# One ordered list for the attention heads: paired value products, roundings through PSUM, experts' loads from ScalarE

## The chip, the cores and the metric

One NeuronCore of a Trainium2 chip. It has five engines with a queue each, which run in order and meet at semaphores: TensorE (PE; its weight loads are a row of their own, PEld), VectorE (DVE), ScalarE (ACT), GpSimd (POOL) and SyncE (SP, which here only issues DMA). TensorE writes its results to PSUM. The metric is device time in microseconds (us), lower is better.

## The reference

Three parts, one after the other: attention over 16 heads (2 batches of 8) of 768 tokens and 64 dimensions; a soft mixture of 8 experts with 4 slots each; a dense feed-forward part from 512 to 2048 to 512.

```python
q_bucket, k_bucket = ...                     # 6 sign bits of q @ proj and k @ proj
scores = np.where(q_bucket == k_bucket, (q @ k.T) / 8, -1e9)
attn = softmax(scores)                       # sums + 1e-9
x = (attn @ v)                               # as (1536, 512)
logits = x @ phi                             # 32 slots
slot_out[e] = relu((softmax0(logits).T @ x)[e] @ w1[e]) @ w2[e]
y = softmax1(logits) @ slot_out
h = y @ w_in;  out = (h / (1 + exp(-1.702 h))) @ w_out
```

`w_in` and `w_out` come as 64-bit floats, which the kernel narrows to 32 bits itself.

## The kernel before

**A head.** Keys and queries of head n lie in `raw[n]`, 128 partitions x 768. For products in the fast 32-bit format (fp32r in the rows) each is split into a rounded part and the rest: `hi2` and `hi1` (L216, L220) have ScalarE write rounded copies of 64 x 768, `hq` (L230) one more, and `lo` (L227) has VectorE subtract a rounded copy from `raw`, with two inputs in SBUF, twice per head. `bits` (L248, L237) makes the bucket bits, which four small DMAs put under the keys and queries.

Scores are made per block `kt` of 128 keys (6 blocks) and half h of the queries (384 columns): `cross` (L337) and `scores` (L344) add two products in one PSUM tile `b`, and ScalarE writes exp into `P` (L345). `av` (L359) multiplies values with P: two products per block, one for each half of the queries, each 64 columns wide, in the two column halves of the array; each runs as two passes ("x4" in the chain). `psum_add` (L353) has GpSimd add up P over the blocks. `amax` (L282, L289) makes the scores of the next head but for their small parts, and VectorE takes the maximum: 12 per head. `mprep`, `mrow`, `mstore` turn the maxima into a row that the next head's `scores` subtract.

Per two heads come the sums of P (`sums`, `recs`: L390, L399), the sum of the values (`vsum2`, L381), and per head turning the result to token order (`xtok`, L443; `xnorm`, L452); per pair of heads `xtrans` (L478) and `logits` (L489). In each head one block of `w_in` is narrowed (`win1` to `win4`): two operations of ScalarE (L123, L128), then L132 and L139 on VectorE in `wn` in SBUF, then a DMA to DRAM. And one tile of 1 MB of the experts' weights is loaded (`load_expert`, L109, from SyncE).

**PSUM.** Tag `A` (2 tiles) holds amax, `B` (3) the scores, `AV` (1) the value products, and `M` (2 tiles, `misc`) all else, in turn: bits, sums, transposes, the row of maxima, logits. A tile of a tag can be written once the tile two (or three) before it in that tag was read.

**The order** is written out: the engines run what the program issues, each in that order. A table P gives tasks a step within the head (6 steps, one per key block); `at` puts them into half steps; the loop at L657 to L685 then issues, for each step, cross and scores of the block, two amax, the value products of the block before, the tasks of the half step, and so on.

**After the heads** the rest of the experts' tiles are loaded into the memory that the attention leaves (18 tiles, SyncE), then come slots, experts (L902, L939) and the feed-forward part, whose products (L1121) run to the end.

Of the kernel before, what the change touches and what calls it, by code (L numbers as in the profile page):

```python
# [52 lines left out]
def build(nc, tc, qk0, qk, v, phi, consts, w1, w2, w_in, w_out, out):  # L53
# [53 lines left out]
    def load_expert(i):  # L107
        wtile[i] = take(F32, f"w{i}")
        SP.dma_start(wtile[i], experts[i])  # L109
# [402 lines left out]
    P = {'b2': 1.4, 'mp1': 3.5, 'mr1': 4.0, 'ms1': 4.8, 'vs0': 3, 'y0': 2.2, 'y1': 5.2, 'y2': 7.5, 'y3': 8.0, 'y4': 8.5, 'hi20': -0.4, 'bits': 0.4, 'hi21': 1.0, 'hi10': 1.5, 'hi11': 2.4, 'lo0': 2.7, 'lo1': 3.0, 'hq': 2.6, 'lr': 3.2, 'mprep': 3, 'mrow': 4, 'mstore': 4.0, 'avout': 0.0, 'vsum': 4.5, 'vsum2': 3.5, 'lv': 0.2, 'sums': 1.8, 'recs': 3.0, 'nom0': 3.5, 'nom1': 4.6, 'xtok0': -2.0, 'xn00': 0, 'xn01': 1.3, 'xtok1': 4.0, 'xn10': 4.6, 'xn11': 5.0, 'xt0': -0.3, 'xt1': 0.5, 'lg': 1.0, 'lw': -0.5, 'w1': 3.8, 'w2': 5.5, 'w3': 5.9, 'w4': 7, 'le': -1.0}  # L512
    todo = {}

    def at(n, s, f, *a):
        todo.setdefault(12 * n + int(2 * s + 24) - 24, []).append((s, f, a))

    for n in range(2, NH):
        e = n - 2
        at(e, P['hi20'], hi2, n, 0)  # L520
        at(e, P['bits' if e else 'b2'], bits, n)
        at(e, P['hi21'], hi2, n, 1)
        e = n - 1
        at(e, P['hi10'], hi1, n, 0)
        at(e, P['hi11'], hi1, n, 1)
        at(e, P['hq'], hq, n)
        at(e, P['lo0'], lo, n, 0)
        at(e, P['lo1'], lo, n, 1)
        at(e, P['lr'], load_raw, n + 2)
    for n in range(1, NH):  # L530
        k = 0 if n < NH - 1 else -1
        at(n - 1, (P['mp1'] if n == 1 else k + P['mprep']), mprep, n)
        at(n - 1, (P['mr1'] if n == 1 else k + P['mrow']), mrow, n)
        at(n - 1, (P['ms1'] if n == 1 else k + P['mstore']), mstore, n)
    for n in range(NH):
        at(n + 1, P['avout'], avout, n)
        at(n, P['lv'], load_v, n + 1)
        if n:
            at(n - 1, P['vsum'], vsum, n)
    for p in range(NH // 2):  # L540
        n = 2 * p
        at(n + 1, P['vsum2'], vsum2, p)
        if p < NH // 2 - 1:
            at(n + 2, P['sums'], sums, p)
            at(n + 2, P['recs'], recs, p)
            at(n + 2, P['nom0'], nomatch, n, nrm)
            at(n + 2, P['nom1'], nomatch, n + 1, nrm)
            at(n + 3, P['xtok0'], xtok, n)
            at(n + 3, P['xn00'], xnorm, n, 0)
            at(n + 3, P['xn01'], xnorm, n, 1)  # L550
            last = p == NH // 2 - 2
            at(n + 3, 2 if last else P['xtok1'], xtok, n + 1)
            at(n + 3, 2.5 if last else P['xn10'], xnorm, n + 1, 0)
            at(n + 3, 3 if last else P['xn11'], xnorm, n + 1, 1)
            at(n + 3, 4 if last else 6 + P['xt0'], xtrans, p, 0)
            at(n + 3, 4.5 if last else 6 + P['xt1'], xtrans, p, 1)
            at(n + 3, 5 if last else 6 + P['lg'], logits, p)
    n = NH - 2
    at(n + 1, 2.5, nomatch, n, None)
# [18 lines left out]
    for j in range(16):  # L578
        e = j - 1
        if j:  # L580
            at(e, P['y0'] if j < 3 else P['lw'], load_win, j)
            at(e, P['y1'] if j < 3 else P['w1'], win1, j)
        for k, f in enumerate((win2, win3, win4)):
            at(e, P[f"{'y' if j < 2 else 'w'}{k + 2}"], f, j)
    for i in range(NWA):
        at(i + 1, P['le'], load_expert, i)

    at(0, P['vs0'], vsum, 0)
    amaxes = {}
    A1 = [2, 2, 2, 3, 3, 3, 4, 4, 4, 4, 5, 5]  # L590
    for n in range(1, NH):
        for i in range(12):
            k = i // 2 if n < NH - 1 or i < 4 else 2 + (i - 4) // 3
            if n == 1:
                k = A1[i]
            if k is not None:
                amaxes.setdefault(6 * (n - 1) - 2 + k, []).append((n, i))

    def do(k):
        for _, f, a in sorted(todo.get(k, []), key=lambda x: (2 * x[0]) % 1):  # L600
            f(*a)
# [55 lines left out]
    for s in range(-2, max(todo) // 2 + 1):  # L657
        n, kt = s // 6, s % 6
        ax = amaxes.get(s, [])
        head = 0 <= n < NH  # L660
        late = kt == 0
        if head:
            cross(n, kt, 0)
            if late:
                cross(n, kt, 1)
            else:
                scores(n, kt, 0)
                psum_add(n, kt, 0)
        early = 2 if s else 0
        for x in ax[:early]:  # L670
            amax(*x)
        if 0 <= s - 1 < 6 * NH:
            av((s - 1) // 6, (s - 1) % 6)
        do(2 * s)
        if head:
            if late:
                scores(n, kt, 0)
            else:
                cross(n, kt, 1)
            scores(n, kt, 1)  # L680
        for x in ax[early:]:
            amax(*x)
        if head and kt > 0:
            psum_add(n, kt, 1)
        do(2 * s + 1)  # L685
# [557 lines left out]
```

## Time and profile before

| | us |
|---|---|
| median of 3 runs | 478.41 (478.35 to 481.0) |
| the profiled execution | 478.17 |
| its span | 476.4 |
| TensorE busy | 461.0 (97%) |
| VectorE busy | 340.1 (71%) |
| ScalarE busy | 289.8 (61%) |
| GpSimd busy | 240.8 (51%) |

The span leaves 1.8 us around it. The granted clock of TensorE is 0.998 of full speed, which is 2.4 GHz. Busy time counts matmuls with their modelled ends, so a busy TensorE may still pause. The attention takes the span from 20 to about 272 us, the experts to 315 us, the feed-forward part the rest. A head takes some 15.6 us. To read a stage, look at the chain of waits in it (what released each step of the chain that ended last) beside the busy time of each engine in it.

### The profile page before, as it was taken

To read this page: it belongs to the slowest core of one execution; us is meant where nothing else is said; L and a number is where in the kernel's file an instruction comes from. 1 tells how busy PE (TensorE), PEld (TensorE's weight loads), DVE (VectorE), ACT (ScalarE), POOL (GpSimd) and SP (SyncE) were. 2 spreads that over 40 slices of the span, in tenths; PEclk is the share of its full clock that TensorE was granted. 3 is DMA by queue.
4 is the path that set the end of the run, shared out by engine and by line. 5 is a ranking of instruction groups with operands and counts; after the bars stand their busy time and mean duration, and the time that the engine had idled before them with its cause. 6 is when DMAs were issued, how large, how long until landed. Compare 5 with 4: busy or idle time off the path is not lost.

```text
span 476.4 us, 7295 instructions
## 1 busy us (share of the span) xinstructions
PE 461.0 (97%) x2457; PEld 287.1 (60%) x2457; DVE 340.1 (71%) x660; ACT 289.8 (61%) x564; POOL 240.8 (51%) x247
## 2 busy tenths in 40 slices
PE   7899999999999999999999999999999999999996
PEld 3645555555555555555545553346778788888885
DVE  3688899898998998989976631459877665544541
ACT  7538867777777777876755320446666665445441
POOL 5466789596795886968957400034464530000000
PEclk9999999999999999999999999999999999999999
DMA  4325655366355643564455599999400003001001
GB/s 146 105 84 189 222 179 165 108 215 214 96 173 182 216 143 120 192 217 147 134 202 193 190 360 419 404 406 423 190 0 1 0 2 132 1 1 66 1 0 66
DMA packets 22024, 75.06 MB, mean 158 GB/s; under 512 B 3210, under 2 KB 8804, under 8 KB 16612
## 3 DMA queue, kind: packets, MB, share of 16 engines
q1 hardware_dynamic: 19672, 70.41, 41.3%
q10 hardware_dynamic: 2316, 4.20, 2.3%
q8 instruction: 19, 0.31, 0.3%
q14 instruction: 17, 0.14, 0.1%
HBM read 64.26 MB, written 7.34 MB: 150 GB/s over the span
## 4 chain that ended last, share of the span: by engine, by line
PE 82%; DVE 14%; issue 2%; ACT 1%; DMA 1%; ACTq 0%; POOL 0%; DVEq 0%
PE o L1121 28%; PE av L359 13%; PE b L337 8%; PE b L344 6%; PE a L282 6%; DVE QK L227 5%; DVE mx L289 5%; PE hp L902 3%; PE sop L939 3%; PE bp L248 3%; PE h L1093 2%; PE xtp L443 1%; PE sm L390 1%; PE lg L489 1%; PE xTp L478 1%
## 5 line engine op out<-in xcount | busy, mean ns | idle before, releaser
L353 POOL TENSOR_TENSOR Ps<-Ps,P 128x384 f32<-128x384 f32 x120 | 135.8, 1151 | 13.1 <-ACT P L345 12.9
L345 ACT ACTIVATE P<-b 128x384 f32<-128x384 f32 x192 | 90.2, 491 | 64.6 <-PE b L344 60.9
L289 DVE TENSOR_REDUCE mx<-a 128x1 f32<-128x384 f32 x192 | 97.3, 545 | 19.8 <-PE a L282 18.9
L1121 PE MATMUL o<-wh,ring 128*128 128x512 f32 x384 | 109.6, 395 | 0.2 <-ACT ring L1107 0.2
L359 PE MATMUL av<-P,v 128*64 128x384 f32 x384 | 91.6, 512 | 0.8 <-ACT P L345 0.7
L1121 PEld LDWEIGHTS o<-wh,ring 128*128 128x128 f32 x384 | 71.0, 188 | 16.5 <-issue 1.8
L337 PE MATMUL b<-QK 128*128 128x384 f32 x192 | 73.0, 393 | 0.0
L1102 DVE TENSOR_TENSOR g<-h,g 128x384 f32<-128x384 f32 x64 | 35.4, 555 | 45.9 <-ACT g L1098 44.4
L344 PE MATMUL b<-QK 97*128 97x384 f32 x192 | 64.1, 347 | 0.0
L337 PEld LDWEIGHTS b<-QK 128*128 128x128 f32 x192 | 35.6, 189 | 38.1 <-issue 38.1
L282 PE MATMUL a<-QK 88*128 88x384 f32 x192 | 55.1, 359 | 3.4 <-DVE mx L289 1.7
L1121 PE MATMUL o<-wl,ring 128*128 128x512 f32 x192 | 55.3, 393 | 0.0
L1098 ACT ACTIVATE g<-h 128x384 f32<-128x384 f32 x64 | 31.2, 491 | 28.2 <-PE h L1093 27.8
L1107 ACT CAST ring<-g 128x384 fp32r<-128x384 f32 x64 | 32.7, 513 | 24.4 <-DVE g L1102 23.7
L353 POOL TENSOR_TENSOR Ps<-P,P 128x384 f32<-128x384 f32 x30 | 29.9, 1003 | 33.8 <-ACT P L345 33.8
L282 PEld LDWEIGHTS a<-QK 88*128 88x128 f32 x192 | 36.4, 194 | 9.1 <-DVE mx L289 5.8
L1121 PEld LDWEIGHTS o<-wl,ring 128*128 128x128 f32 x192 | 35.9, 188 | 9.6 <-issue 1.7
L344 PEld LDWEIGHTS b<-QK 97*128 97x128 f32 x192 | 35.3, 190 | 9.3 <-issue 8.7
L227 DVE TENSOR_TENSOR QK<-raw,QK 64x768 fp32r<-64x768 f32 x28 | 39.8, 1421 | 0.8
L359 PEld LDWEIGHTS av<-P,v 128*64 128x64 f32 x384 | 22.6, 134 | 28.3 <-ACT P L345 15.2
L1112 DVE TENSOR_TENSOR ring<-g,ring 128x384 fp32r<-128x384 f32 x64 | 38.7, 608 | 0.3
L1027 POOL TENSOR_TENSOR wl<-wt,wh 128x512 fp32r<-128x512 f32 x16 | 22.9, 1429 | 31.3 <-ACT wh L1022 31.0
(169 smaller groups left out, 567.5 us busy)
## 6 DMA issues: line engine op xcount, KB each, us to landing
w<-in_w SPq DMA_DIRECT2D x32, 1024.0 KB, 5.0
wif<-in_w_in SPq DMA_DIRECT2D x16, 512.0 KB, 3.8
wof<-in_w_out SPq DMA_DIRECT2D x7, 1024.0 KB, 19.8
raw<-in_qk SPq DMA_DIRECT2D x15, 384.0 KB, 3.0
win<-wn ACTq DMA_DIRECT2D x16, 256.0 KB, 4.0
v<-in_v SPq DMA_DIRECT2D x16, 192.0 KB, 3.9
win<-win SPq DMA_DIRECT2D x3, 1024.0 KB, 12.8
QK<-Bt SPq DMA_DIRECT2D x60, 48.0 KB, 2.7
```

What stands on the lines that cost most here:

```text
L227: (V if n > 1 else G).tensor_tensor(out=q1[r, s, :], in0=raw[n][r, :], in1=hi.bitcast(F32), op=ALU.subtract)
L282: T.matmul(a, q2[0:88, 0, qt * 128 : (qt + 1) * 128], q2[0:88, 1, h * HS : (h + 1) * HS], start=True, stop=True,)
L289: V.tensor_reduce(out=mxs[n][:, qt, h : h + 1], in_=a, axis=AX.X, op=ALU.max)
L337: T.matmul(b, q1[:, 1, kt * 128 : (kt + 1) * 128], q1[:, 0, h * HS : (h + 1) * HS], start=True, stop=False)
L344: T.matmul(b, q2[0:97, 1, kt * 128 : (kt + 1) * 128], q2[0:97, 0, qs], start=False, stop=True)
L345: A.activation(out=Pt[n, kt][:, qs], in_=b, func=AF.Exp, scale=0.125)
L353: e.tensor_tensor(out=Ps[n][:, c], in0=Pt[n, 0][:, c] if kt == 1 else Ps[n][:, c], in1=Pt[n, kt][:, c], op=ALU.add)
L359: T.matmul(avp[n][64 * h : 64 * h + 64, :], vt[n][:, kt, :], Pt[n, kt][:, h * HS : (h + 1) * HS], start=kt == 0, stop=kt == KT - 1,)
L1102: V.tensor_tensor(out=gt[i], in0=hp[i], in1=gt[i], op=ALU.mult)
L1107: A.copy(out=gh[i], in_=gt[i])
L1112: (e or V).tensor_tensor(out=gl[i], in0=gt[i], in1=gh[i].bitcast(F32), op=ALU.subtract)
L1121: T.matmul(op[grp, t], u[i][:, t * 128 : (t + 1) * 128], w[wq][:, wi, :], start=f == 0 and j == 0, stop=f == NF - 1 and j == 2,)
```

## The change

1. `lo` is replaced by `lo1` and `lo2`: ScalarE rounds all 128 partitions of half the columns into a PSUM tile (tag `M`), and VectorE subtracts it from `raw` in two operations of 64 x 384, each with one input in SBUF and one in PSUM. So a head has two roundings of 128 x 384 where it had one `hi1` of 64 x 768, and four subtractions where it had two. `narrow1` of `w_in` writes to a PSUM tile of tag `M` too, and the two roundings on VectorE read it there.
2. The value products of key blocks 0 and 1, and of 4 and 5, are issued back to back.
3. All tasks of a head, cross, scores, amax, value products and sums too, have a place in one list that is sorted by a new table P; the loop is gone. P has 5 buffers instead of 4.
4. The 14 experts' tiles that come during the attention are issued from ScalarE's queue.

```diff
@@ -106,7 +106,7 @@
 
     def load_expert(i):
         wtile[i] = take(F32, f"w{i}")
-        SP.dma_start(wtile[i], experts[i])
+        (A if i < NWA else SP).dma_start(wtile[i], experts[i])
 
 
...
-    def narrow3(dst, f64, c):
+    def narrow3(dst, f64, c, src=None):
...
-            out=d, in0=hi[:, c, :], scalar=-(2**31), in1=d, op0=ALU.bitwise_and, op1=ALU.bitwise_or
+            out=d,
+            in0=hi[:, c, :],
+            scalar=-(2**31),
+            in1=d if src is None else src.bitcast(I32),
+            op0=ALU.bitwise_and,
+            op1=ALU.bitwise_or,
...
+    lot = {}
+
+    def lo1(n, h):
+        lot[h] = pps.tile([128, HS], F32R, name=f"lo{n}_{h}", tag="M", bufs=2)
+        A.copy(out=lot[h], in_=raw[n][:, h * HS : (h + 1) * HS])
+
+    def lo2(n, h):
+        c = slice(h * HS, (h + 1) * HS)
+        for s in range(2):
+            r = QR[s]
+            V.tensor_tensor(
+                out=QK1[n % 2][r, s, c], in0=raw[n][r, c], in1=lot[h][r, :].bitcast(F32), op=ALU.subtract
+            )
...
-            Pt[n, kt] = pq.tile([128, S], F32, name=f"P{n}_{kt}", tag="P", bufs=4)
+            Pt[n, kt] = pq.tile([128, S], F32, name=f"P{n}_{kt}", tag="P", bufs=5)
...
+    wp = {}
+
+        narrow0(wf[j], 0, A)
+        wp[j] = misc([128, 512], f"wp{j}")
+        narrow1(wp[j], wf[j], 0)
...
-        narrow3(wn[j], wf[j], 0)
+        narrow3(wn[j], wf[j], 0, wp[j])
...
-    P = {'b2': 1.4, 'mp1': 3.5, ...}
+    P = {
...
+        "s11": 1.52, "xn01": 1.5784, "lo20": 1.6, "sums": 1.828, "c20": 1.8892, "s20": 2.02, "a1": 2.06, "v0": 2.1,
+        "v1": 2.101, "a11": 2.1167, "lo11": 2.1197, "c21": 2.2278, "hi11": 2.357, "s21": 2.3896, "lo21": 2.424,
...
+    tasks = []
+
+    def put(n, s, f, *a):
+        tasks.append((6 * n + s, len(tasks), f, a))
...
+    for n in range(NH):
+        for kt in range(KT):
+            for h in range(2):
+                put(n, P[f"c{kt}{h}"], cross, n, kt, h)
+                put(n, P[f"s{kt}{h}"], scores, n, kt, h)
+                if kt:
+                    put(n, P[f"p{kt}{h}"], psum_add, n, kt, h)
+            put(n, P[f"v{kt}"], av, n, kt)
...
-    for s in range(-2, max(todo) // 2 + 1):
...
+    for _, _, f, a in sorted(tasks, key=lambda x: x[:2]):
+        f(*a)
```

TensorE, head 5, key blocks 1 and 2, before (b is a score tile with its head, block and half; a is amax of the next head; av the value products; the lines are those of each kernel):

```order
L359 MATMUL av5_1183<-P5_0_1135,v5_956 64x384 x2
L337 MATMUL b5_1_1_1191<-QK1_1_94 128x384
L344 MATMUL b5_1_1_1191<-QK2_2_88 128x384
L337 MATMUL b5_2_0_1198<-QK1_1_94 128x384
L344 MATMUL b5_2_0_1198<-QK2_2_88 128x384
L282 MATMUL a6_8_1203<-QK2_0_93 128x384
L282 MATMUL a6_9_1206<-QK2_0_93 128x384
L359 MATMUL av5_1183<-P5_1_1170,v5_956 64x384 x2
L337 MATMUL b5_2_1_1212<-QK1_1_94 128x384
L344 MATMUL b5_2_1_1212<-QK2_2_88 128x384
L337 MATMUL b5_3_0_1220<-QK1_1_94 128x384
```

and with the change:

```order
L357 MATMUL b5_2_0_1226<-QK1_1_94 128x384
L364 MATMUL b5_2_0_1226<-QK2_2_88 128x384
L302 MATMUL a6_1_1230<-QK2_0_93 128x384
L379 MATMUL av5_1233<-P5_0_1174,v5_974 64x384 x2
L379 MATMUL av5_1233<-P5_1_1201,v5_974 64x384 x2
L302 MATMUL a6_11_1238<-QK2_0_93 128x384
L357 MATMUL b5_2_1_1243<-QK1_1_94 128x384
L364 MATMUL b5_2_1_1243<-QK2_2_88 128x384
L357 MATMUL b5_3_0_1253<-QK1_1_94 128x384
L364 MATMUL b5_3_0_1253<-QK2_2_88 128x384
L302 MATMUL a6_10_1259<-QK2_0_93 128x384
```

The value products of block 0 have moved back to stand beside those of block 1, behind the scores of block 2.

ScalarE in the same stretch of head 5, before (P is exp, with its head and block; the CASTs are roundings, win32 the DMA of the narrowed weights):

```order
L345 ACTIVATE P5_1_1170<-b5_1_0_1171 128x384
L216 CAST QK2_1_86<-raw7_1065 64x768
L509 DMA win32_1_75<-wn5_1074 128x512
L345 ACTIVATE P5_1_1170<-b5_1_1_1191 128x384
L220 CAST QK1_0_89<-raw6_858 64x768
L345 ACTIVATE P5_2_1197<-b5_2_0_1198 128x384
L220 CAST QK1_0_89<-raw6_858 64x768
L345 ACTIVATE P5_2_1197<-b5_2_1_1212 128x384
L230 CAST QK1_0_89<-QK2_0_93 64x768
L345 ACTIVATE P5_3_1219<-b5_3_0_1220 128x384
L345 ACTIVATE P5_3_1219<-b5_3_1_1239 128x384
```

and with the change (lo is the new rounding, w an expert's tile):

```order
L365 ACTIVATE P5_1_1201<-b5_1_0_1202 128x384
L532 DMA win32_1_75<-wn5_1152 128x512
L239 CAST lo6_0_1216<-raw6_887 128x384
L365 ACTIVATE P5_1_1201<-b5_1_1_1214 128x384
L365 ACTIVATE P5_2_1225<-b5_2_0_1226 128x384
L239 CAST lo6_1_1241<-raw6_887 128x384
L225 CAST QK1_0_89<-raw6_887 64x768
L365 ACTIVATE P5_2_1225<-b5_2_1_1243 128x384
L250 CAST QK1_0_89<-QK2_0_93 64x768
L365 ACTIVATE P5_3_1252<-b5_3_0_1253 128x384
L109 DMA w5_1265<-in_w1 128x2048
```

One of the two roundings of L220 has become two (L239) that write a tile of tag `M`, the first of them ahead of the exp that the paired value products wait for, and the expert's load has come into this queue.

## Rows read from the trace of the kernel before

**Rows 1.** the page: busy us, share, instructions; then busy tenths in 40 slices.

```profile
PE 461.0 (97%) x2457; PEld 287.1 (60%) x2457; DVE 340.1 (71%) x660; ACT 289.8 (61%) x564; POOL 240.8 (51%) x247
...
DVE  3688899898998998989976631459877665544541
```

**Rows 2.** windows of two heads: length, PE, PEld, DVE, ACT, POOL busy, granted clock, DMA.

```profile
85.59:116.88 31.29, 31.06 (x170) 17.30 (x171) 28.47 (x57) 23.36 (x45) 24.33 (x26) 1.00 0.52 171
...
179.14:210.29 31.15, 30.92 (x170) 17.16 (x171) 28.34 (x57) 23.53 (x45) 24.53 (x26) 1.00 0.49 168
```

**Rows 3.** the chain of waits inside those windows: start, length (us), what.

```profile
103.03 0.80 PE av L359 x4
103.83 0.37 PE b L337
104.20 0.18 PE b L344
...
105.09 1.42 PE av L359 x4
...
109.00 0.33 PE xtp L443 x3
...
113.57 0.78 PE bp L248 x8
```

**Rows 4.** the timeline, a weight load after a burst: start, length, idle before.

```profile
101.70 0.19 PEld L337 LDWEIGHTS b<-QK 128*128 128x128 f32 x1 [0.60 <-issue]
```

**Rows 5.** the chain of waits: a rounding of VectorE on the path.

```profile
120.81 1.65 DVE QK L227
```

**Rows 6.** the chain of waits behind the attention: 512-column passes of the experts.

```profile
275.54 0.88 PE lg L765 x4
...
284.37 6.14 PE hp L902 x56
```

**Rows 7.** groups by line, VectorE, 60:250 us: xcount, busy us, mean ns.

```profile
L227 DVE TENSOR_TENSOR QK<-raw,QK 64x768 fp32r<-64x768 f32 x26 | 36.6, 1406 | 0.8
L139 DVE SCALAR_TENSOR_TENSOR wn<-wif,wn 128x512 int32<-128x512 int32 x12 | 16.5, 1376 | 0.4
...
L132 DVE SCALAR_TENSOR_TENSOR wn<-wn,wif 128x512 int32<-128x512 int32 x12 | 11.6, 964 | 0.0
...
L493 DVE TENSOR_TENSOR LT<-lg,LT 64x384 f32<-64x384 f32 x4 | 2.2, 553 | 2.7 <-PE lg L489 2.7
```

**Rows 8.** line L227: smallest, median, largest ns.

```profile
L227 DVE TENSOR_TENSOR QK<-raw,QK x28: 951/1553/1653, 43.4 to 247.8; 64x768 fp32r<-64x768 f32 x28
```

**Rows 9.** the chain of waits: roundings of weights, late and in the first heads.

```profile
317.91 0.71 DVE wt L132
...
26.20 1.47 DVE wn L132
...
42.77 0.60 DVE wn L139
```

**Rows 10.** groups by line on ScalarE, 60 to 250 us.

```profile
L345 ACT ACTIVATE P<-b 128x384 f32<-128x384 f32 x145 | 68.2, 491 | 43.0 <-PE b L344 42.5
L220 ACT CAST QK<-raw 64x768 fp32r<-64x768 f32 x24 | 19.9, 831 | 0.6
...
L369 ACT COPY xu<-av 128x384 f32<-128x384 f32 x12 | 5.8, 480 | 2.8 <-PE av L359 2.4
```

**Rows 11.** the experts' loads on SyncE: issue ns, smallest, median, largest.

```profile
L109 SPq DMA_DIRECT2D w<-in_w x14: 387/422/427, 34.9 to 234.8; - x14
```

**Rows 12.** the chain of waits in the last head but one.

```profile
252.86 1.09 PE av L359 x4
...
256.96 1.24 PE av L359 x4
```

**Rows 13.** the tile xtp in 94 to 105 us: first and last start.

```profile
L452 DVE SCALAR_TENSOR_TENSOR x<-xtp,rr,nv x6: 268/269/269, 100.3 to 102.8; 128x64 f32<-128x64 f32 x6
...
L443 PE MATMUL xtp<-cst,xu x3: 273/273/329, 94.3 to 94.6; 128*128 128x128 f32 x3
```

More of the change, by code (lines that the diff above doesn't have):

```diff
@@ L513, in build @@
[L513 removed]
+    P = {
[14 rows of a table added]
+    }
+    tasks = []
+    def put(n, s, f, *a):
+        tasks.append((6 * n + s, len(tasks), f, a))
     def at(n, s, f, *a):
[L516 removed]
+        k = int(2 * s + 24) - 24
+        x = 2 * s - k
+        put(n, k / 2 + (0.12 + 0.3 * x if k % 2 == 0 else 0.1 + 0.38 * x), f, *a)
     for n in range(2, NH):
         e = n - 2
[L520 to L522 removed]
+        put(e, P['hi20'], hi2, n, 0)
+        put(e, P['bits' if e else 'b2'], bits, n)
+        put(e, P['hi21'], hi2, n, 1)
@@ L523, in build @@
         e = n - 1
[L524 to L529, printed above, removed]
+        put(e, P['hi11'], hi1, n, 1)
+        put(e, P['hq'], hq, n)
+        for h in range(2):
+            put(e, P[f'lo1{h}'], lo1, n, h)
+            put(e, P[f'lo2{h}'], lo2, n, h)
+        put(e, P['lr'], load_raw, n + 2)
     for n in range(1, NH):
         k = 0 if n < NH - 1 else -1
-        at(n - 1, (P['mp1'] if n == 1 else k + P['mprep']), mprep, n)
@@ L538, in build @@
+        put(n, P['lv'], load_v, n + 1)
         if n:
-            at(n - 1, P['vsum'], vsum, n)
+            put(n - 1, P['vsum'], vsum, n)
     for p in range(NH // 2):
         n = 2 * p
-        at(n + 1, P['vsum2'], vsum2, p)
+        put(n + 1, P['vsum2'], vsum2, p)
         if p < NH // 2 - 1:
[L544 to L550, printed above, removed]
-            last = p == NH // 2 - 2
[L552 to L557, printed above, removed]
+            put(n + 2, P['sums'], sums, p)
+            put(n + 2, P['recs'], recs, p)
+            put(n + 2, P['nom0'], nomatch, n, nrm)
+            put(n + 2, P['nom1'], nomatch, n + 1, nrm)
+            put(n + 3, P['xtok0'], xtok, n)
+            put(n + 3, P['xn00'], xnorm, n, 0)
+            put(n + 3, P['xn01'], xnorm, n, 1)
+            last = p == NH // 2 - 2
+            put(n + 3, 2.12 if last else P['xtok1'], xtok, n + 1)
+            put(n + 3, 2.6 if last else P['xn10'], xnorm, n + 1, 0)
+            put(n + 3, 3.12 if last else P['xn11'], xnorm, n + 1, 1)
+            put(n + 3, 4.12 if last else P['xt0'], xtrans, p, 0)
+            put(n + 3, 4.6 if last else P['xt1'], xtrans, p, 1)
+            put(n + 3, 5.12 if last else P['lg'], logits, p)
@@ L558, in build @@
     n = NH - 2
-    at(n + 1, 2.5, nomatch, n, None)
+    put(n + 1, P['vsum2'] + 0.01, nomatch, n, None)
     at(n + 1, 3.5, nomatch, n + 1, None)
@@ L580, in build @@
         if j:
-            at(e, P['y0'] if j < 3 else P['lw'], load_win, j)
-            at(e, P['y1'] if j < 3 else P['w1'], win1, j)
+            put(e, P['y0'] if j < 3 else P['lw'], load_win, j)
+            put(e, P['y1'] if j < 3 else P['w1'], win1, j)
         for k, f in enumerate((win2, win3, win4)):
-            at(e, P[f"{'y' if j < 2 else 'w'}{k + 2}"], f, j)
+            put(e, P[f"{'y' if j < 2 else 'w'}{k + 2}"], f, j)
     for i in range(NWA):
[L586 to L590, printed above, removed]
+        put(i + 1, P['le'], load_expert, i)
+    put(0, P['vs0'], vsum, 0)
+    A1 = [0.54, 0.54, 0.54, 1.06, 1.06, 1.54, 2.06, 2.06, 2.54, 2.54, 3.06, 3.06]
     for n in range(1, NH):
         for i in range(12):
-            k = i // 2 if n < NH - 1 or i < 4 else 2 + (i - 4) // 3
+            x = P[f"a{i}"]
             if n == 1:
[L595 to L601, printed above, removed]
+                x = A1[i]
+            elif n == NH - 1 and i >= 4:
+                x = (i - 4) // 3 + (0.06 if (i - 4) % 3 < 2 else 0.54)
+            put(n - 1, x, amax, n, i)
+    for n in range(NH):
+        for kt in range(KT):
+            for h in range(2):
+                put(n, P[f"c{kt}{h}"], cross, n, kt, h)
[3 more added lines that the diff above has]
+            put(n, P[f"v{kt}"], av, n, kt)
     idle[0] = pps.tile([128, 128], F32, name="idle0", tag="AV", bufs=1)
@@ L655, in build @@
     mrow1(1)
-    for s in range(-2, max(todo) // 2 + 1):
[L658 to L685, printed above, removed]
+    for _, _, f, a in sorted(tasks, key=lambda x: x[:2]):
+        f(*a)
     att.close()
```

21 lines of the change are left out of this document (9 added, 12 removed), and 12 rows, old and new, of the table P.

## Prediction

> **What bounds the kernel now.** I began with the page: TensorE is busy 97% of the span, VectorE 71%, but in the first 60% of the span (the attention) VectorE's tenths read 8 and 9, later 4 to 7 [rows 1]. The share over the span thus hides that two engines are near full in the stage that changes. The windows of two heads show it: of 31.2 us VectorE works 28.4, ScalarE 23.5, GpSimd 24.4, and TensorE nearly all [rows 2]; five such windows follow one another with 31.1 to 31.8 us, the first and the fourth stand here. The granted clock is 1.00 in them, so the 2.4 GHz level, and I expect no change there.
>
> Is TensorE really working, or waiting? In the chain of waits a 384-column product takes 0.18 us, a block's value products 0.80, the first full-width product behind them 0.37, bits (and likewise sums and logits) 0.78, three transpositions 0.33 [rows 3]. For two heads: 72 x 0.18 = 13.0; 12 x 0.80 = 9.6; 4 x 0.78 = 3.1; ten returns to full width at 0.37 - 0.18 = 0.19 make 1.9; 15 transposing passes at 0.11 make 1.7; three small products, estimated at 0.2, make 0.6. Sum 29.9, so about 1.3 of 31.2 us are waits. The largest is one value product of 1.42 instead of 0.80 [rows 3]; the others are tenths, some where VectorE is late, as in the stretch where the chain runs over its subtraction of 1.65 us [rows 5].
>
> So TensorE's own work bounds the attention, VectorE is 1.5 us per two heads behind it, and either alone would bring little.
>
> **Part 1: value products in pairs.** The 0.37 is a weight load of 0.19 us that starts only when its product could, after an idle of 0.60 [rows 4], where other loads run under the product before. Entering a burst costs as well: the experts' products, in column parts too, run 56 passes in 6.14 us, 0.877 for eight passes of 512 columns, two to each part of the array [rows 6]. Scaled to 384 columns a block's value products would take 0.66 inside a stream; alone they take 0.80, so 0.14 is the entry. The change has four bursts a head instead of six: per two heads 4 x 0.14 = 0.56. The returns hardly fall: counted in the order, six value bursts are followed by a full-width product before and six after (the rest by the row of maxima, bits, sums or logits), and bits' returns go from two to one: 0.19. Together 0.75, over 8 pairs of heads **6.0 us**. The bounds are 4 x 0.14 alone, 4.5 us, and 4 x (0.14 + 0.19), 10.6 us.
>
> **Part 2: roundings through PSUM, on VectorE.** Two subtractions of 64 x 768 per head, on average 1.406 us [rows 7], become four of 64 x 384. The old one takes 0.951 at best, 1.553 in the middle and 1.653 at worst [rows 8]. For the new one the trace has no row; half of the best is 0.48, half of the worst 0.83, and the nearest (64 x 384, one input in PSUM) is 0.553 [rows 7], which I take. L139 and L132 take 1.376 and 0.964 [rows 7], but 0.60 and 0.71 at other places [rows 9], so I take 0.70 with PSUM, with 0.60 and the old means as ends. VectorE per two heads: 28.4 - 4 x 1.406 + 8 x 0.553 - 2 x (1.376 + 0.964) + 4 x 0.70 = 25.3. At the low end 24.3, at the high end 28.4 - 5.6 + 8 x 0.83 = 29.4.
>
> That the old subtraction has two prices, 0.95 and 1.6, with GpSimd busy 78% of the time, looks like a collision of the two engines in SBUF. The Trainium skill (SBUF — State Buffer, Who interferes with whom) says that a VectorE instruction with two SBUF inputs contends with a GpSimd one that reads SBUF, and one with at most one SBUF input does not. By that rule the new forms always have their low price, which is my sum; were the collision of another kind (any VectorE access beside GpSimd's), the high end of 29.4 holds, and that is rival C.
>
> **On ScalarE**: one rounding of 0.831 less, two of 128 x 384 more. No row writes PSUM from SBUF at this size; half of 0.831 is 0.42, exp 0.491, a copy of that size 0.480 [rows 10], which I take. Two loads are added at 0.422 [rows 11]. 23.5 - 2 x 0.83 + 4 x 0.48 + 2 x 0.42 = 24.6 of about 30: covered on average, because TensorE's work exceeds it; not covered where an exp stands behind it that value products wait for. SyncE loses 14 loads and nobody waited for that queue on the path, so I count no gain; if ScalarE's slack were gone, the loads would cost 14 x 0.42 = 5.9 us.
>
> **Part 3: the order.** The wait of 1.42 - 0.80 = 0.62 and the tenths behind VectorE should mostly go: VectorE drops by 3.1 us, and between the last scores of a block and its value products now stand the products of the block before too. In exchange there is a new wait: the first rounding (`lo1`) stands ahead of the exp for which the first pair waits, and writes a tile of tag M, which in every second head is free only when three more token steps are done by VectorE (0.27 each [rows 13], behind two maxima). I walk that stretch with the row durations: exp ready 0.65 us late for the pair. The second pair waits for an exp behind the two operations on w_in: 0.2. With a few tenths elsewhere I put 0.9 of waits against 1.3 now: 0.4 x 7 pairs = **2.8 us**.
>
> **The ends.** In the first heads VectorE is alone on the path with a rounding of 1.47 [rows 9], which I price at 0.70; with a little less on the maxima, 1.0 us. In the last two heads (no maxima left) five value products take 1.09 to 1.24 instead of 0.80 [rows 12], 1.3 us in all, because each waits for the exp just issued; with pairs the wait is shared, and a further wait of some 0.7 us near the start of the last head should go: 2.0. Together **3.0 us**.
>
> Behind the attention nothing is changed: from 275.5 us [rows 6] to the end 200.9 us remain. The experts' remaining tiles go into memory that the attention leaves, so their loads start earlier with it.
>
> **Sum**: 478.17 (the profiled execution, 0.2 below the median) - 6.0 - 2.8 - 3.0 = 466.4; I say **466 us**. Its own range is 461 to 472, from the bounds of part 1 and waits of 0.4 to 1.5 per two heads.
>
> **Rivals.**
> A, *all waits go*: with VectorE at 25.3 TensorE never stops. 6.0 + 1.3 x 7 + 4 = 19: 459 us, with the upper bound of part 1 down to 455. For it: every other engine has 5 us of slack per two heads. Against it: tag M.
>
> B, *waits take the place of the entry cost*: tag M's two tiles pass to 18 tenants per two heads instead of 12 (four roundings, two w_in blocks). Turns are fixed, so one long tenancy stops the rest; now the token tile lies from 94.3 to 103.1 us, 8.8 us [rows 13]. If waits come to 2.2 per two heads, 6.0 - 0.9 x 7 + 3.0 leaves 2.7: 475.5 us. The Trainium skill (Perfetto Trace Analysis, Identifying Performance Opportunities) says that the same gap repeated on the engine that should be full can mean too little PSUM for the next tile; that would be this rival, and the present trace has no such gap at tag M. For it: in every head bits would also wait until L139 has read the w_in tile. Against it: the new order has the token tile written at the end of a head and read by step 1.6 of the next head's 6, some 4 us.
>
> C, *VectorE stays as slow*: at 29.4 it is as near to the period as today; parts 1 and 3 bring nothing while it is late, and some 1.5 us remain: 477 us. Against it: the two prices of one instruction [rows 8].
>
> D, *slower*: ScalarE becomes the bound through tag M. It runs in order, and at six places per two heads (four roundings, two w_in operations) it now needs a free M tile before the exps behind can run. Its work is 24.6, so it decides once these six waits exceed 30.5 - 24.6 = 5.9 us, 1 us each. At 1.3 us each the period is 24.6 + 7.8 = 32.4: 478.2 - 3.0 + 1.2 x 7 = 484 us; at 1.6 each 497. For it: an 8.8 us tenancy exists. Against it: most tenants are read within a microsecond or two.
>
> **Chances.** Forecast 0.61, A 0.15, B 0.10, C 0.05, D 0.09. One per cent is 4.8 us, about what a measurement can tell here. Faster by more (below 473.6): forecast and A, 0.76. Within: B and C, 0.15. Slower: D, 0.09. The range 457 to 477 leaves out D, half of C and a third of A.
>
> **What would show it.** Right: in the chain, pieces of eight value passes of about 1.46 us; two heads in about 30 us; the subtraction near 0.55 and both roundings near 0.70 with little spread; GpSimd's sums shorter too; the stage from the logits of the experts to the end again 201 us. Wrong: value products of far more than 1.46 behind ScalarE (B, D), roundings on ScalarE with an idle ahead of them that ends with VectorE (tag M), subtractions above 0.8 (C).

## The result, and the profile after it

The changed kernel takes **465.16 us** (median of 4 runs, 464.51 to 467.56), the kernel before beside it 478.68 us (4 runs, 478.35 to 481.0): ratio 0.9716, 95% interval 0.9678 to 0.9754. The forecast was 466 us, range 457 to 477. The profiled execution has a span of 463.2 us, against 476.4. Medians and intervals here and below leave out one execution, at 481.7 us and a lower granted clock (0.984), of the kernel with w_in's rounding in SBUF.

First the page of the changed kernel, in the form of [rows 1]: busy us, share, instructions.

```profile
PE 448.4 (97%) x2457; PEld 288.5 (62%) x2457; DVE 319.6 (69%) x688; ACT 284.4 (61%) x578; POOL 222.0 (48%) x247
```

VectorE and GpSimd have lost some 20 us each for the same results, ScalarE 5. TensorE's share is 97% as before: its busy time fell with the span, from 461.0 to 448.4.

A window of two heads, to be read against [rows 2] (length, then PE, PEld, DVE, ACT, POOL busy, granted clock, DMA):

```profile
112.67:142.50 29.83, 29.71 (x169) 17.46 (x171) 25.79 (x61) 23.26 (x49) 22.01 (x25) 1.00 0.52 177
```

A pair of heads takes 29.8 us instead of 31.3, and the clock is the same. The chain of waits near that window's middle, the counterpart of [rows 3]:

```profile
129.60 1.44 PE av L379 x8
131.04 0.38 PE a L302
```

Eight passes of two blocks take 1.44 us where two times four took 1.60, and the return behind them is 0.38 as before. VectorE's groups, 60 to 235 us, against [rows 7]:

```profile
L245 DVE TENSOR_TENSOR QK<-raw,lo 64x384 fp32r<-64x384 f32 x46 | 25.4, 552 | 1.0
...
L139 DVE SCALAR_TENSOR_TENSOR wn<-wif,wp 128x512 int32<-128x512 int32 x12 | 8.3, 689 | 0.4
L132 DVE SCALAR_TENSOR_TENSOR wp<-wp,wif 128x512 int32<-128x512 int32 x12 | 8.2, 685 | 0.5 <-ACT wp L128 0.5
```

All three cost what the forecast put down (0.553, 0.70, 0.70).

**Where the gain comes from.** The span is 13.2 us shorter, 13.4 up to the experts' logits. Pieces of the chain that stand at the same work in both kernels cut the span. Before: the bits' product of the third head (counted as the order runs), then logits of the first and of the sixth window.

```profile
52.11 0.78 PE bp L248 x8
85.59 0.77 PE lg L489 x4
242.06 0.77 PE lg L489 x4
```

After, the same, and the experts' logits, which stood at 275.54 in [rows 6]:

```profile
52.37 0.78 PE bp L268 x8
82.83 0.82 PE lg L509 x4
231.38 0.77 PE lg L509 x4
262.10 0.88 PE lg L785 x4
```

| stretch | before | after | change | forecast |
|---|---|---|---|---|
| up to the third head's bits | 52.11 | 52.37 | +0.26 | -1.75 |
| to the first logits | 33.48 | 30.46 | -3.02 | -7.3, with the next row |
| five windows of two heads | 156.47 | 148.55 | -7.92 | (in the row above) |
| to the experts' logits | 33.48 | 30.72 | -2.76 | -2.75 |
| from there to the span's end | 200.9 | 201.1 | +0.2 | 0 |

The forecast's 7.3 is six of its eight pairs at 0.75 and its 2.8 of waits; the first row has its 1.0 and a pair, the fourth its 2.0 and a pair. So the sum came out, at 13.2 for 11.8, because the middle (the second and third rows) gave 3.6 us more than forecast and the first heads 2.0 less: two misses of opposite sign, and that is luck. The rows are good to some 0.8 us only, since the new list puts other work around the same piece: the bits stand 2.5 us behind the first product of their head where they stood 1.7, so some 0.8 of the first two rows is the cut's. Counted from the first product of a head to that of the head two later, the first two heads take 27.9 us instead of 30.4, and it is the third and fourth that gain nothing. Those two heads, before, after, and in the fastest version below (461.35 us), in the form of [rows 2]:

```profile
50.44:80.64 30.20, 29.97 (x162) 16.62 (x161) 27.48 (x55) 23.01 (x44) 25.80 (x27) 1.00 0.55 180
```

```profile
47.96:78.18 30.22, 29.07 (x161) 16.97 (x161) 25.01 (x60) 23.26 (x46) 22.47 (x26) 1.00 0.59 194
```

```profile
48.12:76.23 28.11, 28.01 (x162) 16.92 (x161) 25.07 (x60) 22.32 (x45) 22.57 (x26) 1.00 0.59 192
```

With the change TensorE is idle for 1.15 us of them, against 0.1 in the fastest version. What stands there in the chain of waits:

```profile
42.58 0.34 ACTq L109
...
43.00 6.20 DMA wif<-in_w_in
...
50.95 0.86 PE av L379 x2
```

The load of a piece of w_in goes out at 43.00, 0.4 us behind an expert's megabyte, and lands at 49.2; ScalarE, in order, holds the exponentials behind it and the value product waits. In the steady heads a kindred wait is new, on ScalarE (60 to 235 us). The second line is its counterpart in the kernel before (L216, 60 to 250 us), with 0.5 us of idle in all:

```profile
L221 ACT CAST QK<-raw 64x768 fp32r<-64x768 f32 x22 | 18.2, 829 | 6.9 <-DMA raw<-in_qk 6.8
```

```profile
L216 ACT CAST QK<-raw 64x768 fp32r<-64x768 f32 x22 | 18.3, 832 | 0.5
```

### The profile page after: what moved, and what is told of

Same layout as the page of the kernel before. It is cut to its first block, busy times and chain, and to the rows that moved or that the text cites. A ratio compares the mean times of both kernels' runs of the same rounds, so it can differ in the third digit from the quotient of the medians.

```text
span 463.2 us, 7325 instructions
## 1 busy us (share of the span) xinstructions
PE 448.4 (97%) x2457; PEld 288.5 (62%) x2457; DVE 319.6 (69%) x688; ACT 284.4 (61%) x578; POOL 222.0 (48%) x247
## 4 chain that ended last, share of the span: by engine, by line
PE 88%; DVE 5%; DMA 2%; ACT 2%; issue 1%; ACTq 0%; POOL 0%; DVEq 0%
PE o L1141 27%; PE av L379 15%; PE a L302 9%; PE b L357 8%; PE b L364 7%; PE hp L922 3%; PE sop L959 3%; PE bp L268 3%; PE h L1113 2%; PE xtp L463 1%; PE lg L509 1%; DMA wif<-in_w_in 1%; DVE mx L309 1%; PE xTp L498 1%; PE sm L410 1%
## 5 line engine op out<-in xcount | busy, mean ns | idle before, releaser
L373 POOL TENSOR_TENSOR Ps<-Ps,P 128x384 f32<-128x384 f32 x120 | 119.9, 1010 | 23.9 <-ACT P L365 20.9
L309 DVE TENSOR_REDUCE mx<-a 128x1 f32<-128x384 f32 x192 | 102.1, 548 | 21.5 <-PE a L302 20.2
L365 ACT ACTIVATE P<-b 128x384 f32<-128x384 f32 x192 | 85.8, 487 | 43.0 <-PE b L364 41.6
L379 PE MATMUL av<-P,v 128*64 128x384 f32 x384 | 77.0, 503 | 1.0 <-ACT P L365 1.0
L302 PE MATMUL a<-QK 88*128 88x384 f32 x192 | 70.7, 383 | 3.0 <-DVE QK L257 1.4
L357 PE MATMUL b<-QK 128*128 128x384 f32 x192 | 67.4, 366 | 0.2
L364 PE MATMUL b<-QK 97*128 97x384 f32 x192 | 65.2, 353 | 0.0
L373 POOL TENSOR_TENSOR Ps<-P,P 128x384 f32<-128x384 f32 x30 | 29.8, 1004 | 39.7 <-ACT P L365 39.6
L379 PEld LDWEIGHTS av<-P,v 128*64 128x64 f32 x384 | 23.7, 135 | 27.4 <-issue 21.8
L1132 DVE TENSOR_TENSOR ring<-g,ring 128x384 fp32r<-128x384 f32 x64 | 39.8, 624 | 0.3
L1047 POOL TENSOR_TENSOR wl<-wt,wh 128x512 fp32r<-128x512 f32 x16 | 22.6, 1412 | 30.2 <-ACT wh L1042 29.9
L125 POOL TENSOR_SCALAR wof<-wof 128x512 int32<-128x512 uint16 x16 | 11.1, 696 | 44.7 <-DMA wof<-in_w_out 43.6
```

The lines of the kernel that those rows point to most:

```text
L302: T.matmul(a, q2[0:88, 0, qt * 128 : (qt + 1) * 128], q2[0:88, 1, h * HS : (h + 1) * HS], start=True, stop=True,)
L309: V.tensor_reduce(out=mxs[n][:, qt, h : h + 1], in_=a, axis=AX.X, op=ALU.max)
L357: T.matmul(b, q1[:, 1, kt * 128 : (kt + 1) * 128], q1[:, 0, h * HS : (h + 1) * HS], start=True, stop=False)
L373: e.tensor_tensor(out=Ps[n][:, c], in0=Pt[n, 0][:, c] if kt == 1 else Ps[n][:, c], in1=Pt[n, kt][:, c], op=ALU.add)
L379: T.matmul(avp[n][64 * h : 64 * h + 64, :], vt[n][:, kt, :], Pt[n, kt][:, h * HS : (h + 1) * HS], start=kt == 0, stop=kt == KT - 1,)
L1132: (e or V).tensor_tensor(out=gl[i], in0=gt[i], in1=gh[i].bitcast(F32), op=ALU.subtract)
```

## Experiments

My theory: 0.75 us per pair of heads from TensorE's entries and returns, the rest from waits that go because VectorE is shorter; the loads are neutral. The rivals: the list alone did it; or VectorE's speed did; or PSUM waits eat part of it. All times are medians of 4 to 6 executions, taken beside executions of the kernel before at 478.5 to 478.8 us; the last columns come from the logits' lines of each trace (L511 and L513, in the old code 20 lines earlier).

| kernel | us | ratio to before, 95% | first logits copied at | from there to the last logits added |
|---|---|---|---|---|
| before | 478.7 | | 86.4 | 182.7 |
| changed | 465.16 | 0.9678 to 0.9754 | 83.7 | 171.4 |
| before + pairs | 473.32 | 0.9869 to 0.9901 | 85.6 | 178.9 |
| unpaired | 484.29 | 1.0095 to 1.0134 | 89.3 | 184.6 |
| unpaired, later | 476.18 | 0.9937 to 0.9966 | 87.6 | 178.9 |
| low parts in SBUF | 468.68 | 0.9761 to 0.9804 | 85.0 | 173.9 |
| w_in in SBUF | 474.82 | 0.9894 to 0.9950 | 88.1 | 176.6 |
| experts on SyncE | 463.58 | 0.9656 to 0.9734 | 83.9 | 169.8 |
| raw earlier | 471.33 | 0.9809 to 0.9863 | 91.8 | 171.5 |
| first heads | 463.42 | 0.9649 to 0.9714 | 83.5 | 171.2 |
| expert before raw | 503.80 | 1.0496 to 1.0555 | 98.1 | 197.4 |
| expert after raw | 461.35 | 0.9634 to 0.9659 | 81.7 | 170.4 |
| that + w_in in SBUF | 465.33 | 0.9710 to 0.9736 | 81.6 | 173.6 |
| list alone | 493.73 | 1.0288 to 1.0332 | 92.7 | 191.0 |

### The pairs

**Pairs in the old loop.**

```diff
...
-            av((s - 1) // 6, (s - 1) % 6)
+            for k in {1: (0, 1), 2: (2,), 3: (3,), 5: (4, 5)}.get((s - 1) % 6, ()):
+                av((s - 1) // 6, k)
...
-            Pt[n, kt] = pq.tile([128, S], F32, name=f"P{n}_{kt}", tag="P", bufs=4)
+            Pt[n, kt] = pq.tile([128, S], F32, name=f"P{n}_{kt}", tag="P", bufs=5)
```

> The kernel before with the pairing alone: value products of key blocks 0 and 1, and of 4 and 5, in one step of the old loop (five P buffers instead of four), everything else as before. Theory (0.75 us per two heads, saved on TensorE's own time): 472.7 us (478.7 less 6.0). Rival (VectorE at 28.4 of 31.3 us per two heads is as near to the bound, so that a shorter TensorE only waits for it): 476 to 478.7 us. Rival (the bound of 10.6): 468 us.

Measured 473.32 us, 5.4 less: the theory's 6.0 lies within the interval (4.7 to 6.3). But the total hides a miss. Five windows of two heads lie between these two pieces of the chain:

```profile
84.74 0.84 PE lg L489 x4
...
238.98 0.77 PE lg L489 x4
```

They take 154.24 us instead of 156.47: 0.45 per pair and not 0.75. The stretch behind them, to the experts' logits, takes 31.90 instead of 33.48, so 1.58 less, about twice what the theory gives one pair; there, most likely, the joined value products share their waits for the exponentials. In the steady heads VectorE now stands in TensorE's way:

```profile
115.55:146.30 30.75, 30.25 (x167) 17.42 (x167) 27.85 (x57) 23.46 (x45) 24.78 (x25) 1.00 0.52 172
```

VectorE works 27.85 of the 30.75 us, and the chain of waits runs over it from 118.5 to 132.2 us but for 1.1 us, where in the kernel before it did so from 119.7 to 125.3. So the first rival is half right, and the theory's total came out in part by luck.

**Pairs taken out of the list.**

```diff
-        ... "v0": 2.1, ... "v4": 6.114, ...
+        ... "v0": 1.03, ... "v4": 5.53, ...
```

> The changed kernel with one thing undone: the value products of key blocks 0 and 1, and of 4 and 5, stand apart again (block 0 after the exponentials of block 1, block 4 after those of block 5), so that each head has six entries into the two-column-half form instead of four. Theory (an entry 0.14 us and a return 0.19 us that pairing saves, 0.75 us per two heads): the two-head windows lengthen from 29.8 to 30.6 us and the kernel takes 471.2 us (465.2 + 6.0). Rival (the pairing saves nothing by itself, the list did it): 465 to 466 us. Rival (the bound of the forecast, 10.6): 475.8 us.

Measured 484.29, 19 us more: outside everything I had expected. The chain of waits shows that my place for block 0 was a bad one:

```profile
135.57 0.88 ACT P L365 x2
...
136.49 0.87 PE av L379 x4
```

The product stands right behind the scores whose exponentials it needs, and TensorE waits 0.9 us for them. So I moved it half a step.

```diff
-        ... "v0": 1.03, ...
+        ... "v0": 1.53, ...
```

> The changed kernel unpaired once more, with the product of key block 0 half a step later than in the run before (behind the second scores of key block 1, at 1.53 instead of 1.03 of its head), where its exponentials have ended. Theory (an entry and a return cost 0.33 us, and the other 13 us of the first unpaired run were TensorE standing for the exponentials of block 0, about 1 us a head): 471 to 473 us. Rival (the pairing is worth 19 us in this order because VectorE is no longer near the bound, so that all that TensorE does counts): 480 us or more.

Measured 476.18, 11.0 us more than paired: 8.1 of the 19 were that wait, and the rest is twice what the pairs are worth in the old loop. One reason is VectorE in the old loop, seen above. Another shows in the chain of this kernel, and below it the old kernel's.

```profile
119.37 0.80 PE av L379 x4
120.16 0.78 PE sm L410 x8
...
134.47 0.80 PE av L379 x4
135.26 0.37 PE b L357
```

```profile
129.23 0.80 PE av L359 x4
130.03 0.78 PE bp L248 x8
```

In the old order some bursts of value products ran straight into other work in narrow parts (bits) or into the row of maxima, so splitting or joining them moved no return. In the list three of the four split pairs per two heads have full-width products on either side of both halves: each of these splits costs an entry of 0.16 and a return of 0.19, together 1.05. The fourth runs straight into the sums (119.37) and costs little, and the value product at 145.24 takes 1.08, so 0.28 more; 1.33 in all. The chain from logits to logits is 117.86 to 149.00 us in the unpaired list, 31.14, and 29.86 paired (112.67 to 142.53): 1.28. How much of the factor of two goes to either reason no run separates.

### The roundings

**Low parts of Q and K back in SBUF.**

```diff
+        put(e, P['lo10'], hi1, n, 0)
...
-            put(e, P[f'lo1{h}'], lo1, n, h)
-            put(e, P[f'lo2{h}'], lo2, n, h)
+            put(e, P[f'lo2{h}'], lo, n, h)
```

> The changed kernel with the low parts of Q and K taken as before: one VectorE subtraction per half from two SBUF inputs, the rounded part from SBUF. Theory (a subtraction with two SBUF inputs runs at about 1.4 to 1.6 us beside GpSimd and one with a PSUM input does not): line 227's operation is back at 1.4 us or more, VectorE's busy time in a two-head window rises from 25.8 to about 27 us, and, since it is not the bound, its longer operations cost 0.1 to 0.4 us of waits per pair: 466 to 468 us. Rival (VectorE's speed was what the gain in the steady heads came from): at least 3 us more, 468 to 472. Rival (two PSUM buffers fewer in use by the low parts take away waits): 465 or below.

Measured 468.68, 3.5 more: just above the theory's range and at the foot of the first rival's. Groups between 84 and 236 us:

```profile
L373 POOL TENSOR_TENSOR Ps<-Ps,P 128x384 f32<-128x384 f32 x80 | 84.6, 1074 | 7.4 <-ACT P L365 5.8
...
L302 PEld LDWEIGHTS a<-QK 88*128 88x128 f32 x121 | 22.8, 189 | 16.7 <-issue 6.1 <-DVE mx L309 5.2 <-DVE QK L232 3.0
L232 DVE TENSOR_TENSOR QK<-raw,QK 64x768 fp32r<-64x768 f32 x20 | 20.9, 1046 | 1.4 <-ACT QK L225 0.9
```

The old subtraction runs at 1.05 us here, not at 1.4 to 1.6, and VectorE's sum per two heads moves only from 25.8 to 26.1 us. TensorE's maxima products now wait 3.0 us for it. A window takes 30.20 instead of 29.83 us, 0.37 longer, the upper end of the theory's 0.1 to 0.4: not through a subtraction of 1.4 us or more, as I had it. That it costs because it comes in one piece of 768 columns is my reading; no run shows it, since the edit also takes four tenants per two heads out of tag M and changes ScalarE's roundings.

**Rounding of w_in back in SBUF.**

```diff
-        wp[j] = misc([128, 512], f"wp{j}")
-        narrow1(wp[j], wf[j], 0)
+        if j:
+            wn[j] = scratch([128, 512], F32, f"wn{j}", "wn")
+        narrow1(wn[j], wf[j], 0)
...
-        narrow2(wp[j], wf[j], 0)
+        narrow2(wn[j], wf[j], 0)
...
-        narrow3(wn[j], wf[j], 0, wp[j])
+        narrow3(wn[j], wf[j], 0)
```

> The changed kernel with the second and third step of the rounding of w_in back in SBUF, in place, at the same places of the list. Theory: the two steps are back at 0.96 and 1.4 us beside GpSimd, VectorE gets 1.7 us more per two heads, and waits of 0.1 to 0.3 us per pair come back; but in the first heads a PSUM buffer of the group M is no longer held from the first step to the third: 464.5 to 467.5 us. Rival: VectorE becomes the bound again, 468 us or more.

Measured 474.82, 9.7 more: the rival's side. The two operations are slow again:

```profile
L139 DVE SCALAR_TENSOR_TENSOR wn<-wif,wn 128x512 int32<-128x512 int32 x16 | 21.2, 1328 | 0.5
L132 DVE SCALAR_TENSOR_TENSOR wn<-wn,wif 128x512 int32<-128x512 int32 x16 | 16.4, 1027 | 8.0 <-ACT wn L128 8.0
```

But the chain of this kernel runs over transfers:

```profile
46.16 7.01 DMA win<-wn
...
108.23 7.87 DMA raw<-in_qk
```

A store of the last piece that the next rounding waits for and raw loads that take almost 8 us (and, at 28.71, a load of w_in of 7.21). To tell those from VectorE's own share, the loads had to be moved first.

### The loads

**Experts' loads on SyncE again.**

```diff
-        (A if i < NWA else SP).dma_start(wtile[i], experts[i])
+        SP.dma_start(wtile[i], experts[i])
```

> The changed kernel with all experts' loads issued by SyncE again. Theory (the loads are hidden in the steady heads, the issuing engine costs ScalarE 0.4 us per load off the path): 464.5 to 466 us, no difference. Rival (SyncE's queue holds the loads of raw and w_in behind the expert's, as in the old kernel): up to 2 us more through later raw loads, 467 us. Rival (in the first heads the expert's load no longer stands ahead of that of w_in by its own queue): 464 us.

Measured 463.58, below all that I had put down. The interval overlaps that of the changed kernel, so a gain of 1.6 us is likely but not proved; it lies in the steady heads, not in the first. ScalarE's wait for raw between 60 and 235 us falls from 6.8 to 1.5 (total, times, longest):

```profile
ACT QK L221 <- DMA raw<-in_qk: 1.5, 2, 0.9
```

The place in the list is the same, but the load goes out at another time. Here are the expert's load and the raw load in one head, first in the changed kernel, then in this one (SPq and ACTq are the queues of SyncE and ScalarE):

```profile
102.26 0.34 ACTq L109 DMA_DIRECT2D w<-in_w  x1
103.21 0.33 SPq L194 DMA_DIRECT2D raw<-in_qk  x1
```

```profile
101.55 0.43 SPq L109 DMA_DIRECT2D w<-in_w  x1
103.42 0.33 SPq L194 DMA_DIRECT2D raw<-in_qk  x1
```

Between 60 and 130 us the megabyte goes out 0.95 to 1.0 us ahead of raw from ScalarE, and 1.9 to 4.2 us ahead from SyncE, so that raw, as I read it, meets less of it.

**The raw load earlier.** The dictionary's place `"lr"` goes from 3.70 to 2.55.

> The changed kernel with the load of raw of the head after next issued right after the last read of its buffer (at 2.55 of the head instead of 3.70). Theory (ScalarE's rounding of a head waits up to 1.6 us for that load, six times, 6.8 us in all, and half of it or less reaches TensorE through the exponentials): 463 to 465 us. Rival (the wait is covered): 465 us.

Measured 471.33, 6 us more. The raw load cannot start earlier, since it waits on SyncE until the last low part has read its buffer; in the steady heads nothing changes (171.5 against 171.4). In the first heads, though, the load of w_in now stands behind that wait in SyncE's queue, and lands 8 us after its issue:

```profile
44.60 7.81 DMA wif<-in_w_in
```

That wait is paid twice. TensorE works only 1.99 of the 6 us from 48 to 54, and then runs at half its clock (granted clock 0.50, the 1.2 GHz level):

```profile
54.00:60.00 6.00, 5.86 (x18) 3.00 (x19) 3.36 (x6) 2.99 (x6) 1.00 (x1) 0.50 0.10 33
```

**The first heads closed up.**

```diff
-        ... "y3": 8.2348, "y4": 10.3141,
+        ... "y3": 6.4, "y4": 7.4,
...
-            put(e, P['y0'] if j < 3 else P['lw'], load_win, j)
+            put(e, P['y0'] if j < 2 else 0.6 if j < 3 else P['lw'], load_win, j)
```

> The changed kernel with the first heads' roundings of w_in closed up (third step at 6.4 instead of 8.2, its store at 7.4 instead of 10.3, the load of the third piece at 0.6 instead of 2.96 of its head). Theory (in the second head the rounding waits for a load that is issued only at 43.0 us behind an expert's load and lands at 49.2, and TensorE with it for 1.0 to 2.5 us): 463 to 464 us. Rival (the first heads are bound by loads in any order): 465 us.

Measured 463.42, on the theory, but the interval overlaps that of the changed kernel. The stall for w_in is gone and one for raw, behind the same expert's load, is next:

```profile
44.70 6.48 DMA raw<-in_qk
```

**The expert's load before or after the raw load**, both with the edit above: `"le"` from -2.497 (3.5 of a head's six steps, raw at 3.70) to -4.4 (1.6) or to -1.3 (4.7).

> The same with the expert's load behind the raw load (at 4.7 of the head). Theory: as with the load ahead, 459 to 462 us. Rival (behind raw the expert's load delays the small transfers of the row of maxima and of the bits, and TensorE waits for these): 464 us or more. Rival (the issue on ScalarE, not the transfer, is what costs, since SyncE's issue saved 1.6 us): 463.4 us.

> The changed kernel with the first heads' roundings of w_in closed up and the expert's load issued 1.9 of a step earlier in each head (at 1.6 instead of 3.5, where 3.7 is the place of the raw load). Theory (the load of raw takes 6 to 8 us because the 1 MB of the expert's goes ahead of it; free of that it lands in 3 to 4 us, and ScalarE's waits for raw, 9.2 us in all, go, of which a part reaches TensorE): 459 to 462 us. Rival (raw is late because its buffer comes free late, not because of the expert's load): 463.4 us, as with the first heads alone.

Behind the raw load: **461.35 us**, interval clear of the changed kernel's, 3.8 us faster than it and the fastest here. Of these, 2.1 are over the version with the first heads closed up alone, whose interval still touches this one's. Raw takes 3.1 us to land in the middle, and ScalarE no longer waits for it between 60 and 235 us, though ScalarE still issues the expert's load. So those waits came from the megabyte going out just ahead of raw; the issuing engine matters, as far as the runs show, through the time at which it sends the load. The gain lies in the first heads (2.0 us) and the steady ones (1.0).

```profile
raw<-in_qk SPq DMA_DIRECT2D x15, 384.0 KB, 3.1
```

Ahead of it: 503.80 us, 40 us more than with the first heads closed up alone. The expert's load now meets the bits, four transfers of 48 KB for which the maxima wait:

```profile
114.50 7.63 DMA QK<-Bt
...
124.46 0.32 PE b L364
...
125.74 1.31 PE av L379 x4
```

This I had not thought of; raw itself did land in 3.3 us, so the theory on raw held and the price was elsewhere. A large part of that price is TensorE's clock, which falls to half behind such waits (the last section shows one): the mean granted clock of the profiled execution is 0.951 over 503.4 us, so by an estimate up to some 25 us of the 40.

### The rounding of w_in, without the transfers

The edit of the rounding above, in the version of 461.35 us.

> The rounding of w_in back in SBUF once more, now in the version that took 461.35 us (the first heads' roundings closed up, the expert's load behind the raw load). Theory (of the 10 us that the rounding in SBUF cost before, most was transfers: raw loads that went out later behind a longer VectorE and landed behind the expert's megabyte, 7.2 to 7.9 us each, and in the first heads a store that the next rounding waited for; VectorE's own part is 0.1 to 0.3 us per pair): 462 to 464.5 us. Rival (the 1.0 and 1.3 us operations themselves hold up the maxima and low parts that TensorE waits for): 468 us or more.

Measured 465.33, 4.0 more than 461.35: between theory and rival. So of the 9.7 about 6 came with the transfers; 4.0, or 0.5 per pair, are left for VectorE's longer operations. A window of two heads here, and then of the version of 461.35 us:

```profile
80.81:110.86 30.05, 29.92 (x169) 17.39 (x171) 27.39 (x61) 23.00 (x48) 23.16 (x25) 1.00 0.53 176
```

```profile
80.87:110.50 29.63, 29.50 (x170) 17.45 (x171) 25.82 (x61) 22.94 (x48) 22.00 (x25) 1.00 0.55 179
```

And what the weight loads of the maxima products wait for (60 to 240 us: total, times, longest), in the same order:

```profile
PEld a L302 <- DVE mx L309: 13.4, 33, 1.0
```

```profile
PEld a L302 <- DVE mx L309: 5.7, 13, 0.8
```

VectorE rises by 1.6 us to 27.4 of 30: 2.7 short of the window's length, and its maxima are late 33 times instead of 13.

### The list alone

All four undone together (low parts, w_in, experts' loads, pairs apart at 1.03 and 5.53).

> The ordered list alone: the changed kernel with the pairing, the low parts through PSUM, the rounding of w_in through PSUM and the experts' loads on ScalarE all undone. Theory (waits 2.8 us, last heads 2.0 us, part of it only with the cheaper VectorE operations): 473 to 477 us. Rival (the parts need one another, the list without the cheap VectorE operations is no better than the old steps): 478 us or more.

Measured 493.73: the rival. With block 0 at 1.53 it would be some 485.6 (493.7 less the 8.1 between the two unpaired runs, an estimate). By itself the list, with the places that were fitted to the new operations, is no better than the old loop, and probably 7 us worse; a list fitted to the old operations was not tried. From the changed kernel, the four single undoings add 19.1 + 3.5 + 9.7 - 1.6 = 30.7 us, all at once 28.6: from this side the parts nearly add.

## Why the prediction was right, and where it was not

**Part 1, pairs: the cost was right, the total partly luck.** A pair of bursts takes 1.44 us (forecast 1.46), and the returns behind value products did not fall, as counted. The forecast was 6.0, and 5.4 were measured in the old loop, but there a steady pair gave 0.45 instead of 0.75, with VectorE in the way, and the ends gave the rest. In the list the pairs are worth 11.0, next to the upper bound of 10.6, an entry and a return for each: three of four splits do move a return there, and a wait of 0.28 comes on top.

**Part 2, VectorE: prices right, total a little low.** 0.552, 0.689 and 0.685 us against 0.553 and 0.70; 25.8 per two heads instead of 25.3. The new forms have a low price with little spread beside GpSimd. The Trainium skill (SBUF — State Buffer, Who interferes with whom) says that a VectorE instruction with at most one SBUF input, outside the 2-port modes, does not contend with GpSimd. The trace agrees: the subtractions take 0.545 to 0.558 us and the roundings 0.676 to 0.700, and GpSimd's sums are faster too.

```profile
L373 POOL TENSOR_TENSOR Ps<-Ps,P 128x384 f32<-128x384 f32 x120 | 119.9, 1010 | 23.9 <-ACT P L365 20.9
```

They took 1.151 us in the kernel before, and 1.074 with the low parts back in SBUF. The first sum of a head, of two P, is less regular: 1.003 before, 1.004 now, 1.198 with the low parts back. But I took the old subtraction's 1.4 us for its price in any order; in the list it is 1.05. Rival C falls.

**ScalarE and tag M: rivals B and D fall.** It works 22.6 to 23.3 us per two heads, issues not counted (with two of 0.34 some 24, forecast 24.6). The waits that I foresaw there did not come: ScalarE was idle ahead of all 28 low roundings together for 0.8 us.

```profile
L239 ACT CAST lo<-raw 128x384 fp32r<-128x384 f32 x28 | 13.6, 487 | 0.8 <-DVE QK L245 0.4
```

A repeated gap on the engine that should be full, which by the Trainium skill (Perfetto Trace Analysis, Identifying Performance Opportunities) can mean too little PSUM, is not in this trace: TensorE works 29.71 of the 29.83 us of the window above.

**Part 3, waits: direction right, size low, and its name wrong.** Forecast 0.4 per pair, and a pair gave 1.58 where 0.75 + 0.4 were forecast. Four joined bursts account for 4 x 0.16 = 0.64 and the return behind the bits for 0.19, so waits for some 0.75: by the prediction's own count, of the 1.3 per window some 0.6 are left instead of 0.9. Tag M's wait stayed away. But I put that gain to the order; the list alone loses, and wins only with the operations it is made for.

**The first heads: the step that failed.** Forecast -1.0 with VectorE's rounding of 1.47 us gone, and a pair's gain from there on. The rounding went (0.685 now), and the first two heads did shorten, by 1.6 to 2.4 us according to the cut. But I had not walked the loads behind them: the third and fourth heads gained nothing (30.22 us for 30.20), because the piece of w_in behind the expert's megabyte held up the exponentials; with the loads moved they take 28.11. **Loads from ScalarE at no gain and no cost** failed with it: their place, 0.2 of a step ahead of raw, cost 2 to 4 us. What counts is how far ahead of raw the megabyte goes out, which the place and the issuing engine both set.

**The last heads: right in size** (-2.76 for 2.75, to within the cut's 0.8). Pairs alone in the old loop gave 1.58 of it; the split of the rest, between the pair's own gain, shared waits and the wait near the last head's start, is only argued.

**Slips in the working.** With both bounds at once its own range would begin at 458 and not at 461; rival D's 497 is 496 by its own sum; and the 0.60 of [rows 9] is the part of a rounding of 0.68 us that stood on the chain, so the low end for the roundings should be 0.68. None of them moves the forecast.

## To carry to other kernels

A transition cost depends on the neighbours as well as on the instruction: count which bursts already touch other narrow work before you price joining them. When an order is fitted to certain operations, test the parts by undoing each one in the new order as well as by doing it alone in the old; the two prices differed here by a factor of two. When a total comes out, cut the span and see whether each stretch did. And before a bulk load is moved, list the smaller transfers in flight around its new place, since here those, not the bulk load, were what engines waited for.

## What the runs showed of the hardware

A load of 384 KB that went out about 1 us behind a megabyte took 6.48 and 7.87 us; with the megabyte behind it, it takes 3.1 in the middle. One of 48 KB took 7.63 beside a megabyte, where its median in these traces is 1.9 to 2.7. A stall of TensorE can be paid twice. With the expert's load ahead of raw, the chain of waits lies on that transfer from 114.5 to 122.1 us; TensorE still has work until 117.6, then stands for 2.0 us, and from about 120 to 126.8 its granted clock is at half, the 1.2 GHz level. A product there takes 0.32 instead of 0.18 us and a block's value products 1.31 instead of 0.80. The standstill, and the stretch at half clock but for its first 2 us:

```profile
117.64:119.66 2.02, 0.00 (x1) 0.04 (x1) 0.56 (x2) 1.08 (x4) 1.92 (x4) 1.00 0.68 238
122.17:127.00 4.83, 4.83 (x16) 3.28 (x16) 3.50 (x11) 1.97 (x4) 0.85 (x1) 0.53 0.09 36
```
